# Moving tiles in SBUF: the right heap to 64 modulo 512 bytes, six K and Q buffers to unequal offsets

## The chip, the cores and the metric

One core of a Trainium2 chip runs one program per execution. The metric is the device time in microseconds of that execution, the median over several. TensorE, VectorE, ScalarE and GpSimd each have an instruction queue of their own and meet through semaphores; SyncE issues most DMAs. SBUF has 128 partitions; a tile's address is a byte offset inside each partition, and it is these offsets that the change alters.

## What is computed

One transformer-like block on x of 2048 rows and 448 columns, in float32:

```python
mod = (_silu(c) @ w_mod).reshape(c.shape[0], 6, 1, -1)
sa, ca, ga, sb, cb, gb = (mod[:, 0], mod[:, 1], mod[:, 2], mod[:, 3], mod[:, 4], mod[:, 5])
h = _layernorm(x, axis=-1) * (1 + ca) + sa
x = x + ga * _A_ref(h, A_wqkv, A_wo)
h = _layernorm(x, axis=-1) * (1 + cb) + sb
x = x + gb * _B_ref(h, B_w_in, B_w_sp, B_b_sp, B_w_out)
return x
```

A is attention with 16 heads of 28 columns and a softmax over all 2048 keys. B is a gated MLP: z = gelu(h w_in) is split in two halves of 896 columns, z1 and z2; z2 is normalised over its columns, multiplied along the rows by the 2048x2048 matrix w_sp, shifted by b_sp, multiplied by z1 and projected back to 448 columns by w_out.

## The kernel before

**Matmuls.** TensorE streams a moving operand of up to 512 columns against weights of 128 columns that it has loaded before. Operands are float32r. To keep precision, most are split in a high part and a low remainder, and a product is made of several matmuls: 11 steps for a 448-row contraction (the pairs in STEPS), three for the spatial product and for the output projection. In the attention, K and Q carry both parts on different rows, so that one matmul of 84 or 86 rows does it all.

**Tiles and where they stand.** Pools allocate from the left end of SBUF upward or, with side="right", from the right end downward. heapD (84 KB per partition, L67) is the first and topmost tile on the right. It holds in turn: hT (the first normalised input, transposed) and wqk (weights of the Q and K projection); OT (the attention's output) and wos; w2, most of z2, and uT (the gated result). Below it on the right lie the stage tiles (qf, qh, ql, osb, rb) and, early, wv. On the left lie the constants (ident, ones, spread and small ones), V, the early loads, and for the attention the pool stk with the six buffers kst0 to kst2 and qst0 to qst2 of 8 KB each (L329), then npool and ppool with the probabilities P. After the attention the left holds heapA (w1, later z2), heapB (h2T, later z2), two more heaps, and the tiles of w_sp (wsp_h, wsp_l). Each allocation is rounded up to 32 bytes, so that a tile's address is the sum of the sizes before it.

**Stages, in the order of time.**
1. To about 92 us: modulation, first layer norm, V (v_tiles, L261: weights from hT, moving wv) and the first Q and K projections (qk_unit, L270: weights wqk, moving hT).
2. To 165 us: the remaining 20 units of L270, with one m product (below) put before steps 1, 4, 7 and 10 of each.
3. To 893 us: attention. The loop runs over u = 16 heads x 16 key tiles. For each u it issues four s products (s_mm, L420: weights a 128-key slice of K, moving a 512-query slice of Q), each followed by an m product (m_mm, L389: weights a 128-query slice of Q, moving a 512-key slice of K) for the unit 20 ahead, hence for the next head or the one after. VectorE takes the row maximum of each m result (L394), ScalarE the exponential of each s result into P (L424). After every second u come eight products with V (pv_mm, L435). Head h uses kst and qst number h mod 3. The ring of seven PSUM tiles is shared by s and m. The last 20 u have no m products any more.
4. Normalisation of a head: its output is copied to osb (tag qf, two buffers), the sums are inverted, osb is scaled and scattered to OT by DMAs (n_scatter, L472). The last head goes another way: a matmul with spread as weights spreads its sums (L673), and VectorE inverts and scales (L675, L676).
5. To 938 us: output projection (wo_mm, L600: weights OT, moving wos), second layer norm. To 1012 us: z1 (L712: weights w1 in heapA, moving h2T). To 1083 us: z2 (L774: weights h2T, moving w2 in heapD).
6. To the end: the spatial product in four blocks of 512 columns (mix_part, L820 to L822: weights the 128-column slices of z2, 8 of 16 tiles in heapD, 4 each in heapA and heapB; moving wsp_h, wsp_l, wsp_h), and between its steps the projection of the block before (y_part, L860 to L862: weights uT in heapD, moving wouts).

The order on each engine is written out by hand (the schedule is manual); tiles only wait for the last use of the slot that they take.

Of the kernel before, what the change touches and what calls it, by code (L numbers as in the profile page):

```python
# [8 lines left out]
F32 = mybir.dt.float32  # L9
F32R = mybir.dt.float32r  # L10
# [6 lines left out]
S, D, H, DH, FH = 2048, 448, 16, 28, 896  # L17
# [16 lines left out]
def tile_adaln_mha_gmlp(ctx, tc, x, wqkv, wo, w_in, w_spT, b_sp, w_out, cT, w_mod, out):  # L34
    nc = tc.nc
    ctx.enter_context(tc.manual_schedule())
    pe, dve, act, pool, sp = nc.tensor, nc.vector, nc.scalar, nc.gpsimd, nc.sync

    const = ctx.enter_context(tc.tile_pool(name="const", bufs=1))
    dpool = ctx.enter_context(tc.tile_pool(name="dpool", bufs=1, side="right"))  # L40
# [8 lines left out]
    ident = const.tile([128, 128], F32, name="ident")  # L49
    make_identity(nc, ident)  # L50
    ones = const.tile([128, 128], F32, name="ones")
    dve.memset(ones, 1.0)

    spread = const.tile([128, 128], F32, name="spread")
    dve.tensor_copy(
        spread.rearrange("p (a b) -> p a b", b=32),
        ident.rearrange("p (a b) -> p a b", b=32)[:, :, 28:29].broadcast_to([128, 4, 32]),
    )
    mhalf = const.tile([128, 4], F32, name="mhalf")
    dve.memset(mhalf, -0.5)  # L60
    silu = const.tile([112, 4], F32, name="silu")
# [3 lines left out]
    bcs = {"gb": const.tile([128, D], F32, name="bc_gb")}  # L65

    heapD = dpool.tile([128, 24 * 896], F32R, name="heapD")  # L67

    def hview(heap, off, a, b):
        return heap[:, off : off + a * b].rearrange("p (a b) -> p a b", b=b)  # L70
# [11 lines left out]
    def weight_part(dst, i, raw, hi_eng, lo_eng, zero=True):  # L82

        n = raw.shape[-1]
        h = dst[:, i if i < 3 else 6, :n]
        if hi_eng is act:
            act.activation(h, raw, AF.Copy)
        else:
            hi_eng.tensor_copy(h, raw)
        if i < 3:  # L90
            sub(lo_eng, dst[:, 3 + i, :n], raw, h)
        else:
            sub(lo_eng, dst[0:64, 7, :n], raw[0:64], h[0:64])
            if zero:
                pool.memset(dst[64:128, 7, :n].bitcast(F32), 0.0)
# [6 lines left out]
    def ln_transpose(xns, full_pool, dsts, scol, bcol, engs, los=(pool,) * 4, mid=None, after=None):  # L102

        tps = []
        for c in range(4):
            tp = ring.tile([128, 512], F32, name="tp", tag="s")
            tps.append(tp)
            for t in range(4):
                pe.transpose(tp[:, t * 128 : (t + 1) * 128], xns[t][:, c * 128 : (c + 1) * 128], ident)  # L109
        if mid:  # L110
            mid()
        for c in (0, 2, 1, 3):
            tp = tps[c]
            f = full_pool.tile([128, 512], F32, name="hfull")
            if engs[c] is act:
                act.activation(f, tp, AF.Identity, scale=scol[:, c : c + 1], bias=bcol[:, c : c + 1])
            else:
                engs[c].tensor_scalar(
                    out=f, in0=tp, scalar1=scol[:, c : c + 1], scalar2=bcol[:, c : c + 1], op0=ALU.mult, op1=ALU.add
                )  # L120
            hi = dsts[:, c if c < 3 else 6, :]
            if engs[c] is act:
                act.activation(hi, f, AF.Copy)
            else:
                engs[c].tensor_copy(hi, f)
            if c < 3:
                sub(los[c], dsts[:, 3 + c, :], f, hi)
            else:
                sub(los[c], hi[64:128], f[64:128], hi[64:128])
            if after:  # L130
                after(c)
# [9 lines left out]
    stage = stg.enter_context(tc.tile_pool(name="stage", bufs=2, side="right"))  # L141
# [12 lines left out]
    def load_mod(pair, eng):  # L154
        for k in range(4):
            wms[pair, k] = e1.tile([112, 2, D], F32, name="wm", bufs=4)
            eng.dma_start(wms[pair, k], w_mod[:, pair, k])

    def load_x(g, eng):
        xg = e1.tile([128, 4, D], F32, name="xg")  # L160
        for t0, t1 in ((0, 1), (1, 2), (2, 4)) if g == 0 else ((0, 4),):
            eng.dma_start(xg[:, t0:t1, :], x[g, :, t0:t1])
        for t in range(4):
            xts[4 * g + t] = xg[:, t, :]
# [60 lines left out]
    def ln_stats(g):  # L225
        mv = e1.tile([128, 4, 2], F32, name="mv")
        sts = []
        for t in range(4):
            st = e1.tile([128, 6], F32, name="st", bufs=4)
            dve.bn_stats(out=st, in_=xts[4 * g + t])  # L230
            sts.append(st)
        for t in range(4):
            dve.bn_aggr(out=mv[:, t, :], in_=sts[t])
        rs = e1.tile([128, 4], F32, name="rs")
        rstd_of(mv[:, :, 1], rs, 4)
        mv1[g] = (mv, rs)
# [19 lines left out]
    def v_tiles(*kts):  # L256
        pvs = [ring.tile([128, 512], F32, name="pv", tag="s") for _ in kts]
        for j, (a, b) in enumerate(STEPS):
            for kt, pv in zip(kts, pvs):
                g, t = divmod(kt, 4)  # L260
                pe.matmul(pv[:, :D], hT[g][:, a, t * 128 : (t + 1) * 128], wv[:, b, :], start=j == 0, stop=j == NST - 1)  # L261
        for kt, pv in zip(kts, pvs):
            dve.tensor_copy(V[:, kt, :, 0:DH], pv[:, :D].rearrange("p (h d) -> p h d", d=DH))

    def qk_unit(m, g, mid=None):
        pq = ring.tile([128, 512], F32, name="pq", tag="s")
        for j, (a, b) in enumerate(STEPS):
            if mid and j in mid:
                mid[j]()
            pe.matmul(pq, wqk[:, b, m * 128 : (m + 1) * 128], hT[g][:, a, :], start=j == 0, stop=j == NST - 1)  # L270
        f = stage.tile([128, 512], F32, name="qf")
        act.activation(f, pq, AF.Copy)  # L272
        hi = stage.tile([128, 512], F32R, name="qh")
        act.activation(hi, f, AF.Copy)
        lo = stage2.tile([128, 512], F32R, name="ql")
        sub(pool, lo, f, hi)
        for i, t in enumerate((hi, lo)):
            sp.dma_start(qk_scr[i][m * 128 : (m + 1) * 128, g * 512 : (g + 1) * 512], t.bitcast(F32))
# [42 lines left out]
    for g in range(NG):  # L321
        if g + 2 < NG:
            load_x(g + 2, sp)
        if g in (0, 2):
            load_mod(1 + g // 2, sp)
        if g == 3:
            early.close()
            stk = att.enter_context(tc.tile_pool(name="stk", bufs=1))
            kq = [[stk.tile([128, S], F32R, name=f"{n}st{i}") for n in "kq"] for i in range(3)]  # L329
            kst, qst = [a[0] for a in kq], [a[1] for a in kq]  # L330
            npool = att.enter_context(tc.tile_pool(name="npool", bufs=2))

            def load_head(h, c0=0, c1=S):
                k, q = kst[h % 3], qst[h % 3]
                if h < 2 and c0 == 0:
                    pool.memset(k[64:86, :].bitcast(F32), 1.0)
                for r0, i in ((0, 0), (56, 1), (28, 0)):
                    sp.dma_start(k[r0 : r0 + 28, c0:c1].bitcast(F32), qk_scr[i][D + h * DH : D + (h + 1) * DH, c0:c1])
                for r0, i in ((0, 0), (28, 1), (56, 0)):
                    sp.dma_start(q[r0 : r0 + 28, c0:c1].bitcast(F32), qk_scr[i][h * DH : (h + 1) * DH, c0:c1])  # L340

            load_head(0, 0, 1536)
            for m in (0, 3):
                qk_unit(m, g)
            load_head(0, 1536, S)
        if g == 0:
            v_tiles(0, 1)
            v_tiles(2)
        else:
            v_tiles(4 * g)  # L350
            v_tiles(4 * g + 1)
        if g == 0:
            for i in range(4):
                weight_part(wqk, i, raws.pop(("qk", i)), act, (dve, pool)[i % 2], False)
        if g + 1 < NG:
            ln_transpose(xns, e1, hT[g + 1], cols["ca"], cols["sa"], (act,) * 4)
        if g + 2 < NG:
            ln_stats(g + 2)
            xns = ln_norm(g + 2)
        if g > 0:  # L360
            v_tiles(4 * g + 2)
        else:
            pool.memset(V[:, :, :, DH:32], 1.0)
        v_tiles(4 * g + 3)
        if g == 2:
            mod_bc("ga", accs[1][:, 0, :])
            mod_col(("sb", accs[1][:, 1, :], 0.0))
        if g < 3:
            for m in (0, 3):
                qk_unit(m, g)  # L370
        if g in (1, 2):
            for k in range(4):
                mod_acc(g, k)
# [289 lines left out]

    HELD = 7
    x_load(0)
    for i in range(4):
# [11 lines left out]
    for i in range(2):  # L680
        win_prep(0, i, pool)
    for t in range(1, HELD):
        wo_mm(t, STEPS_MAIN)
    for qb in range(4):
        o_split(3, qb, dve if qb % 2 == 0 else pool)
    for i in range(2, 4):
        win_prep(0, i, pool)
    for t in range(HELD):
        wo_mm(t, STEPS_Z)
# [247 lines left out]
```

## Time and profile before

| | us |
|---|---|
| median of 3 runs | 1469.54 (1468.12 to 1470.2) |
| the profiled execution | 1468.3 |
| its span, first to last instruction | 1466.5 |
| granted TensorE clock | 0.999 of full |
| TensorE busy | 1440.9 |
| VectorE busy | 882.5 |
| ScalarE busy | 733.0 |

How to read what follows. In groups of instructions the number behind the comma is the mean duration of one in ns, behind the bar the idle time before them. Matmuls overlap: the next one starts before the recorded end of the last, so the distance between starts says more than a duration. In the chain in order of time a row is start, length, engine, tile, line and a count. In the view of one line, three numbers with slashes are minimum, median and maximum duration in ns. PEld rows are weight loads; q behind an engine's name means its queue.

### The profile page before, as it was taken

How to read it: one execution, taken by the hardware profiler on the slowest of the kernel's cores; microseconds unless marked ns; L12 is line 12 of the kernel's file. 1: busy time of each engine (PE TensorE's matmuls, PEld its weight loads, DVE VectorE, ACT ScalarE, POOL GpSimd, SP SyncE). 2: the span in 40 equal slices, each digit the busy share in tenths (PEclk: the TensorE clock that was granted, in tenths of full speed). 3: DMA queues.
4: the chain of work that ended last, by engine and by line, in shares of the span. 5: the costliest groups of instructions: out<-in, count | busy, mean ns of one | idle time of the engine just before them, and what ended most of it. 6: DMA issues, size and time to landing. Idle time of an engine off the chain costs nothing.

```text
span 1466.5 us, 19636 instructions
## 1 busy us (share of the span) xinstructions
PE 1440.9 (98%) x7314; PEld 1016.6 (69%) x7314; DVE 882.5 (60%) x1440; ACT 733.0 (50%) x1390; POOL 301.3 (21%) x273
## 2 busy tenths in 40 slices
PE   6999999999999999999999999999999999999999
PEld 5887655555555555555555556888988888888887
DVE  6657888888888888888888823911542411414114
ACT  3523576776776776777677695542432201212111
POOL 5734200000011012001000012511663400302002
PEclk9999999999999999999999999999999999999999
DMA  7563401221022221221112005332003422313223
GB/s 214 149 179 146 137 19 36 52 53 40 17 50 53 54 51 28 52 53 46 34 27 52 15 24 165 139 141 86 15 21 96 127 69 77 101 65 96 81 69 107
DMA packets 56132, 111.24 MB, mean 76 GB/s; under 512 B 11900, under 2 KB 22780, under 8 KB 53516
## 3 DMA queue, kind: packets, MB, share of 16 engines
q1 hardware_dynamic: 55868, 109.76, 25.5%
q8 instruction: 57, 0.93, 0.3%
q14 instruction: 39, 0.32, 0.1%
q10 hardware_dynamic: 168, 0.23, 0.1%
HBM read 75.89 MB, written 29.48 MB: 72 GB/s over the span
## 4 chain that ended last, share of the span: by engine, by line
PE 94%; DVE 2%; DMA 2%; issue 1%; POOL 1%; SPq 0%; ACT 0%; DVEq 0%; POOLq 0%; ACTq 0%
PE st_ps L420 18%; PE mt L389 16%; PE o_ps L435 16%; PE acc L820 7%; PE acc L822 7%; PE acc L821 7%; PE pq L270 5%; PE z_ps L774 5%; PE z_ps L712 5%; PE pv L261 2%; PE y_ps L861 2%; PE y_ps L862 2%; PE y_ps L860 2%; PE tp L109 1%; DMA wm<-in_w_mod_dram 1%
## 5 line engine op out<-in xcount | busy, mean ns | idle before, releaser
L394 DVE TENSOR_REDUCE pm<-mt 128x1 f32<-128x512 f32 x1024 | 632.3, 683 | 121.0 <-PE mt L389 120.6
L424 ACT ACTIVATE P<-st_ps 128x512 f32<-128x512 f32 x1024 | 514.2, 621 | 153.6 <-PE st_ps L420 153.2
L420 PE MATMUL st_ps<-qst,kst 86*128 86x512 f32 x1024 | 410.4, 412 | 0.0
L389 PE MATMUL mt<-kst,qst 84*128 84x512 f32 x1024 | 405.8, 396 | 0.3 <-DVE pm L394 0.3
L420 PEld LDWEIGHTS st_ps<-qst,kst 86*128 86x128 f32 x1024 | 192.9, 189 | 145.1 <-issue 82.1
L435 PE MATMUL o_ps<-P,V 128*32 128x512 f32 x2048 | 247.5, 599 | 0.0
L389 PEld LDWEIGHTS mt<-kst,qst 84*128 84x128 f32 x1024 | 194.9, 190 | 37.2 <-DVE pm L394 0.7
L76 DVE TENSOR_TENSOR wsp_l<-raw_sp,wsp_h 128x512 fp32r<-128x512 f32 x64 | 52.2, 818 | 188.7 <-ACT wsp_h L757 188.7
L757 ACT ACTIVATE wsp_h<-raw_sp 128x512 fp32r<-128x512 f32 x64 | 40.3, 630 | 233.7 <-DMA raw_sp<-in_w_spT_dram 189.7
L435 PEld LDWEIGHTS o_ps<-P,V 128*32 128x32 f32 x2048 | 54.2, 109 | 123.5 <-issue 116.2
L76 POOL TENSOR_TENSOR heapD<-u,heapD 128x512 fp32r<-128x512 f32 x27 | 44.7, 1690 | 258.0 <-ACT heapD L839 172.9
L461 POOL TENSOR_TENSOR osb<-osb,rb 128x512 f32<-128x512 f32 x15 | 19.2, 1279 | 353.2 <-ACT P L424 191.8
L270 PE MATMUL pq<-heapD 128*128 128x512 f32 x308 | 87.4, 402 | 2.9 <-DVE heapD L76 2.9
L820 PE MATMUL acc<-wsp_h,heapD 128*128 128x512 f32 x224 | 89.1, 398 | 0.7 <-DVE u L837 0.7
L822 PE MATMUL acc<-wsp_h,heapD 128*128 128x512 f32 x224 | 88.6, 396 | 0.0
L821 PE MATMUL acc<-wsp_l,heapD 128*128 128x512 f32 x224 | 88.2, 394 | 0.0
L270 PEld LDWEIGHTS pq<-heapD 128*128 128x128 f32 x308 | 59.2, 193 | 17.1 <-DVE heapD L76 3.4
L76 POOL TENSOR_TENSOR nl<-nf,nh 16x128 fp32r<-16x128 f32 x16 | 7.2, 450 | 281.2 <-issue 149.1
L865 DVE TENSOR_TENSOR x2t<-x2t,y_ps 128x448 f32<-128x448 f32 x12 | 7.5, 621 | 75.9 <-PE y_ps L862 75.9
L272 ACT ACTIVATE qf<-pq 128x512 f32<-128x512 f32 x28 | 16.7, 597 | 66.9 <-PE pq L270 66.9
L820 PEld LDWEIGHTS acc<-wsp_h,heapD 128*128 128x128 f32 x224 | 42.1, 188 | 10.9 <-DVE u L837 1.8
L822 PEld LDWEIGHTS acc<-wsp_h,heapD 128*128 128x128 f32 x224 | 42.1, 188 | 10.4
(150 smaller groups left out, 1686.0 us busy)
## 6 DMA issues: line engine op xcount, KB each, us to landing
raw_sp<-in_w_spT_dram SPq DMA_DIRECT2D x64, 256.0 KB
kst<-qk_scr SPq DMA_DIRECT2D x45, 224.0 KB
qst<-qk_scr SPq DMA_DIRECT2D x45, 224.0 KB
qk_scr<-qh SPq DMA_DIRECT2D x28, 256.0 KB
qk_scr<-ql SPq DMA_DIRECT2D x28, 256.0 KB
z_scr<-z1t SPq DMA_DIRECT2D x28, 256.0 KB
z<-z_scr SPq DMA_DIRECT2D x28, 256.0 KB
wm<-in_w_mod_dram SPq DMA_DIRECT2D x12, 392.0 KB
```

The lines of the kernel that those rows point to most:

```text
L76: eng.tensor_tensor(out=dst, in0=a, in1=hi.bitcast(F32), op=ALU.subtract)
L270: pe.matmul(pq, wqk[:, b, m * 128 : (m + 1) * 128], hT[g][:, a, :], start=j == 0, stop=j == NST - 1)
L389: pe.matmul(mt, qst[h % 3][0:84, t * 128 : (t + 1) * 128], kst[h % 3][0:84, kb * 512 : (kb + 1) * 512], start=True, stop=True)
L394: dve.tensor_reduce(out=pms[h][:, t, kb : kb + 1], in_=mt, axis=AX.X, op=ALU.max)
L420: pe.matmul(st, kst[h % 3][0:86, kt * 128 : (kt + 1) * 128], qst[h % 3][0:86, qb * 512 : (qb + 1) * 512], start=True, stop=True)
L424: act.activation(p, st, AF.Exp, scale=SCALE)
L435: pe.matmul(otile[h][32 * qb : 32 * qb + 32, :], V[:, kt, h, :], ptiles.pop((u, qb)), start=kt == 0, stop=kt == NT - 1)
L712: pe.matmul(ps_t, w1[:, b, f * 128 : (f + 1) * 128], h2T[g][:, a, :], start=j == 0, stop=j == NST - 1)
L774: pe.matmul(ps_t[:, :D], h2T[g][:, a, tt * 128 : (tt + 1) * 128], w2[:, b, hf * D : (hf + 1) * D], start=j == 0, stop=j == NST - 1)
L820: pe.matmul(acc[f], z2[st][:, 0, fs], hi, start=st == 0, stop=False)
L821: pe.matmul(acc[f], z2[st][:, 0, fs], lo, start=False, stop=False)
L822: pe.matmul(acc[f], z2[st][:, 1, fs], hi, start=False, stop=st == NT - 1)
```

## The change

spread is no longer a constant but takes a qf slot of the stage pool, and the copy that fills it stands just before the last part of the attention's tail. A tile of 416 bytes that nothing uses is put behind heapD, which lowers heapD and all that stands below it on the right by as much. The six K and Q buffers come in another order, with unused tiles of 256, 64, 32 and 32 bytes between them. No instruction but the copy is moved; sizes and values stay the same.

```diff
@@ -50,12 +50,6 @@
-    spread = const.tile([128, 128], F32, name="spread")
-    dve.tensor_copy(
-        spread.rearrange("p (a b) -> p a b", b=32),
-        ident.rearrange("p (a b) -> p a b", b=32)[:, :, 28:29].broadcast_to([128, 4, 32]),
-    )
@@ -65,6 +59,7 @@
     heapD = dpool.tile([128, 24 * 896], F32R, name="heapD")
+    dpool.tile([128, 104], F32, name="padD")
@@ -326,8 +321,12 @@
             stk = att.enter_context(tc.tile_pool(name="stk", bufs=1))
-            kq = [[stk.tile([128, S], F32R, name=f"{n}st{i}") for n in "kq"] for i in range(3)]
-            kst, qst = [a[0] for a in kq], [a[1] for a in kq]
+            kq = {}
+            for i, (nm, pad) in enumerate((("k0", 64), ("q0", 0), ("q2", 16), ("k2", 0), ("q1", 8), ("k1", 8))):
+                if pad:
+                    stk.tile([128, pad], F32, name=f"pad{i}")
+                kq[nm] = stk.tile([128, S], F32R, name=f"{nm[0]}st{nm[1]}")
+            kst, qst = ([kq[f"{n}{i}"] for i in range(3)] for n in "kq")
             npool = att.enter_context(tc.tile_pool(name="npool", bufs=2))
@@ -663,6 +662,12 @@
+    spread = stage.tile([128, 512], F32, name="spread", tag="qf")[:, 0:128]
+    dve.tensor_copy(
+        spread.rearrange("p (a b) -> p a b", b=32),
+        ident.rearrange("p (a b) -> p a b", b=32)[:, :, 28:29].broadcast_to([128, 4, 32]),
+    )
     HELD = 7
```

## The prediction

> **What bounds the kernel now.** I read the page first, for which engine ends the time.
>
> ```profile
> span 1466.5 us, 19636 instructions
> ...
> PE 1440.9 (98%) x7314; PEld 1016.6 (69%) x7314; DVE 882.5 (60%) x1440; ACT 733.0 (50%) x1390; POOL 301.3 (21%) x273
> ...
> PEclk9999999999999999999999999999999999999999
> ...
> PE 94%; DVE 2%; DMA 2%; issue 1%; POOL 1%; SPq 0%; ACT 0%; DVEq 0%; POOLq 0%; ACTq 0%
> ```
>
> TensorE is on the chain that ended last for 94% of the span, at the full granted clock. The change adds and removes no matmul. So the question is whether one matmul follows the last any sooner when its operands stand at other addresses. That needs the distance from one start to the next, which the chain in order of time gives. First z1 and z2:
>
> ```profile
> 957.63 54.90 PE z_ps L712 x242
> 1012.53 70.43 PE z_ps L774 x352
> ```
>
> 54.90/242 = 0.2269 us for 512 columns, 70.43/352 = 0.2001 us for 448. Nothing in this trace holds a steadier or lower pace, so I call these the floors. Now the spatial product of the gMLP, three matmuls (L820 to L822) per 128x512 tile; the rows are each third matmul, the first two and the last of a stretch with weights from heapD, then the ends of one with weights from heapB:
>
> ```profile
> 1082.95 0.24 PE acc L820
> 1083.65 0.24 PE acc L820
> ...
> 1121.45 0.24 PE acc L820
> ```
>
> ```profile
> 1440.21 0.23 PE acc L820
> ...
> 1444.97 0.23 PE acc L820
> ```
>
> Over heapD it is 38.50/55 = 0.700 us for three, over heapB 4.76/7 = 0.680 us. Same instructions, same moving tiles, same engines around them: only the place of the weights differs. A third of 0.020 us is 6.7 ns per matmul. I call that one slip.
>
> Where do the operands stand? Adding up tile sizes in the order of allocation (each rounded up to 32 bytes): heapA, heapB, the later heaps, wsp_h and wsp_l are at 64 modulo 512 bytes; heapD at 480 (the change's words give 64 after, and padD is 104 x 4 = 416 bytes lower); all six K and Q buffers at 320, which is 64 modulo 256. Every slice taken as weights begins a multiple of 512 bytes on, so it keeps its buffer's offset. 480 is not a multiple of 64; 64 and 320 are.
>
> **The change: heapD.** Recorded ends lie about 0.16 us beyond the next start (390 ns recorded against a step of 227), so differences of recorded durations are differences of pace. Groups by line and shape, mean ns behind the comma:
>
> ```profile
> L820 PE MATMUL acc<-wsp_h,heapD 128*128 128x512 f32 x224 | 89.1, 398 | 0.7 <-DVE u L837 0.7
> L822 PE MATMUL acc<-wsp_h,heapD 128*128 128x512 f32 x224 | 88.6, 396 | 0.0
> L821 PE MATMUL acc<-wsp_l,heapD 128*128 128x512 f32 x224 | 88.2, 394 | 0.0
> L820 PE MATMUL acc<-wsp_h,heapA 128*128 128x512 f32 x112 | 43.7, 390 | 0.0
> L861 PE MATMUL y_ps<-heap,heapD 128*128 128x448 f32 x112 | 41.2, 368 | 0.0
> L774 PE MATMUL z_ps<-heapD,heapB 128*128 128x448 f32 x176 | 35.4, 363 | 0.0
> ```
>
> Lines as minimum/median/maximum ns, L270 before and after line 389 joins it, L389 in the second stretch:
>
> ```profile
> L600 PE MATMUL wo_ps<-heapD x176: 358/368/767, 893.1 to 938.5; 128*128 128x448 f32 x176
> L261 PE MATMUL pv<-wv,heapD x176: 358/367/474, 23.0 to 92.4; 128*128 128x448 f32 x176
> L270 PE MATMUL pq<-heapD x44: 387/389/504, 73.5 to 83.4; 128*128 128x512 f32 x44
> L270 PE MATMUL pq<-heapD x219: 387/395/744, 94.0 to 164.6; 128*128 128x512 f32 x110
> L389 PE MATMUL mt<-kst,qst x80: 393/401/497, 94.6 to 164.8; 84*128 84x512 f32 x80
> ```
>
> Moving data from heapD costs nothing (L774 runs at its floor of 363 with w2 there); weights from heapD do. After the change they stand where heapA's stand:
>
> - acc: (8 + 6 + 4) ns x 224 = 4.0 us; I take 3.9 for the 390 that is sometimes 391.
> - y: three lines at about 5 ns x 112 each = 1.6 us.
> - wo: 5 ns x 176 = 0.9, of which some 65 run before 908 us beside the wait for the last head's normalisation and are worth nothing: 0.6.
> - pv: 4 ns x 176 = 0.7, less the first ones that wait for loads: 0.6.
> - Q/K projection with m products between: 6 ns x 220 = 1.3, and m there 401 against 396 later, 5 ns x 80 = 0.4: 1.7.
>
> Sum **8.4 us**, nearly all on TensorE's own chain. One row speaks against it: L270 in 73.5 to 83.4 us takes weights at 480 with a median of 389, the floor. There weights and moving operand share the offset; in acc they don't (64 against 480). So an odd weight address by itself is not enough, and the y, wo and pv terms, whose offset differences do not change into acc's new one, could come to nothing (5.6 us left). If it were the differences of 0 and 256 that cost in wo, z2 would get these and lose 5 ns x 352 = 1.8 us (3.8 left). I keep 8.4, because the rows with weights at 64 (acc over heapA and heapB, z1, z2) never show a slip.
>
> **The change: K and Q.** From the sizes the buffers go to 64 (k0, q0), 128 (q2, k2), 160 (q1) and 192 (k1) modulo 256. The s product of a head streams its Q while the m product's weights, Q of the next head or the one after, are loaded; m streams a later K while K of the head is loaded. All these pairs have equal offsets now and unequal ones afterwards.
>
> ```profile
> L389 PE MATMUL mt<-kst,qst x1024: 389/396/497, 94.6 to 850.4; 84*128 84x512 f32 x171
> L420 PE MATMUL st_ps<-qst,kst x880: 392/396/506, 199.9 to 839.5; 86*128 86x512 f32 x176
> L420 PEld LDWEIGHTS st_ps<-qst,kst x880: 185/190/195, 200.1 to 839.8; 86*128 86x128 f32 x176
> L420 PE MATMUL st_ps<-qst,kst x55: 388/393/502, 861.7 to 887.0; 86*128 86x512 f32 x55
> L420 PEld LDWEIGHTS st_ps<-qst,kst x53: 186/188/190, 861.9 to 886.7; 86*128 86x128 f32 x53
> ```
>
> ```profile
> 336.82 0.40 PE L389 MATMUL mt<-kst,qst 84*128 84x512 f32 x1
> ...
> 340.09 0.39 PE L389 MATMUL mt<-kst,qst 84*128 84x512 f32 x1
> ```
>
> The last fence is one train of s and m: 14 steps in 3.27 us, 0.2336 each, again one slip over 0.2269. Nothing in the trace shows K and Q at unequal offsets, so I bound it. Best: every slip goes, 6 to 6.7 ns x some 1,900 (without those that open a train) = 12 us gained. Worst: a second slip each, 2,048 x 6.7 = 13.7 us lost; the pair "m, then projection" at unequal offsets has 401, nearly two slips. Between: where s runs alone (861.7 us on) the offsets are just as equal, yet it runs at 393 and its weight loads at 188 instead of 190. So about half the excess needs no change of offset to vanish, and offsets can be blamed for the other half, 6 us. Weights from q1, at 160, would again stand off a multiple of 64; they feed a third of the m products, a sixth of all. 5/6 of 6 is **5 us**, which I take: near the middle of ends far apart.
>
> ```profile
> L394 DVE TENSOR_REDUCE pm<-mt 128x1 f32<-128x512 f32 x1024 | 632.3, 683 | 121.0 <-PE mt L389 120.6
> L424 ACT ACTIVATE P<-st_ps 128x512 f32<-128x512 f32 x1024 | 514.2, 621 | 153.6 <-PE st_ps L420 153.2
> ```
>
> Both consumers sit idle waiting for these products, 121 and 154 us in total, so neither becomes late by a gain of 5 to 12 us. P moves by 128 bytes; V's weight slices stand 128 bytes apart by head, so P meets the same set of differences as before: nothing.
>
> **The change: spread.** It leaves VectorE's start and comes back before the last head's sums.
>
> ```profile
> L55 DVE COPY spread<-ident x1: 573/573/573, 1.3 to 1.3; 128x128 f32<-128x128 f32 x1
> 872.65 6.41 SPq L472 DMA_DIRECT2D heapD<-osb  x8
> 894.81 0.40 PEld L673 LDWEIGHTS sums<-osb,spread 128*128 128x128 f32 x2
> 896.12 3.36 DVE L675 RECIPROCAL rb<-sums 128x512 f32<-128x512 f32 x1 [31.28 <-PE sums L673]
> ```
>
> At the start VectorE then waits for ScalarE's first result anyway: nothing. At the end the copy adds a wait: its slot was osb of head 14, free when the eight scatters issued from 872.65 to 879.06 have landed. Only the reciprocal is queued behind it on VectorE, idle for 31.28 us and waiting for sums at 895. The 0.57 us has some 14 us of cover: nothing. Without that cover it would be 0.6 us straight on the way to the last scatter.
>
> **Sum.** 8.4 + 5 = 13.4 us. The profiled execution took 1468.3 us (1.8 around its span): 1454.9. The median of the runs is 1.2 above it: **1456 us**.
>
> **The rivals.**
> - K and Q lose every slip, as acc over heapA shows for products with company: 1469.5 - 8.4 - 12 = 1449. For it: z2 runs at its floor with unequal offsets. Against it: s alone at 393.
> - K and Q gain nothing, with q1's weights paying up to 5 ns x 320 = 1.6: 1461 to 1463. For it: z1 and acc over heapA have equal offsets and no slip, so equality isn't the fault; rows of 84 and 86 in turn could be.
> - Slower: unequal offsets cost K and Q a second slip, as in "m, then projection" (401): 1469.5 - 8.4 + 13.7 = 1475. It decides from 8.4/2,048 = 4.1 ns per product.
> - The change does not do what it says: the slip comes from something else that goes with heapD, and the time stays at 1469.5. For it only the floor of L270 at 480.
>
> The Trainium skill, SBUF — State Buffer, Who interferes with whom, says that PE never waits on anyone and names only the port pair of VectorE and GpSimd as contended. By that rule the sum is nothing and this last rival holds. The trace disagrees as far as 0.700 against 0.680 goes.
>
> **How the numbers follow.** Forecast (K and Q gain 2 to 9; 1451 to 1460) 0.36; every slip gone 0.22; K and Q unmoved 0.27; second slip 0.09; no effect 0.06. The range takes the first three, out to 1447 and 1465, which leaves 0.15 or a little more outside. A measurement tells some 0.2% (2.9 us) from no change. Faster: the first three, 0.85; same: no effect and a hair of the others, 0.07; slower: 0.08.
>
> **What would show it.** L820 to L822 over heapD at 390 and 0.68 us for three; y at 363; wo, pv near 363; L270 beside L389 near 390; z2 still 363. If y and wo keep 368 while acc falls, the difference of offsets counts, not the weights' own. L389 and L420 at about 393 for the forecast, 390 for the first rival, 396 for the second, 402 for the slower one. L389 with weights from q1 slower than from q0 and q2 would confirm the multiple of 64. I am wrong altogether if L820 over heapD stays at 398.

## The result and the profile after

| | before | after |
|---|---|---|
| median of 20 runs each, same chip, us | 1469.01 (1467.33 to 1471.68) | 1466.32 (1464.62 to 1469.84) |
| ratio after / before | | 0.9984 [0.9977, 0.9991] |
| the profiled execution, us | 1468.3 | 1466.46 |

Faster, by 2.7 us and not by 13: the direction was right, and the time lies 1.3 us above the range. From here on lines are those of the kernel after: pv L256, pq L265, m L388, s L419, wo L599, z1 L717, z2 L779, acc L825 to L827, y L865 to L867.

The page of after: TensorE still ends the time, at the full granted clock.

```profile
span 1464.7 us, 19637 instructions
...
PE 1436.5 (98%) x7314; PEld 1015.3 (69%) x7314; DVE 884.6 (60%) x1440; ACT 733.1 (50%) x1390; POOL 302.0 (21%) x273
...
PEclk9999999999999999999999999999999999999999
...
PE 92%; DVE 2%; POOL 2%; DMA 2%; issue 1%; ACT 0%; SPq 0%; ACTq 0%; DVEq 0%; POOLq 0%
```

The chain in order of time (start, length, line, count):

```profile
960.23 54.87 PE z_ps L717 x242
1015.10 71.34 PE z_ps L779 x352
1086.43 0.23 PE acc L825
1087.13 0.23 PE acc L825
...
1123.85 0.23 PE acc L825
```

The spatial product over heapD now does its three in (1123.85 - 1086.43)/55 = 0.680 us instead of 0.700. z1 is as it was. But z2, which stood at its floor, takes 71.34 us for the same 352 products instead of 70.43.

Groups by line and shape (mean ns behind the comma), then single lines (minimum/median/maximum ns; L265 and L388 are the stretch from 96 to 167 us, L419 the one with m between and then alone):

```profile
L825 PE MATMUL acc<-wsp_h,heapD 128*128 128x512 f32 x224 | 87.6, 391 | 0.6 <-DVE u L842 0.6
L827 PE MATMUL acc<-wsp_h,heapD 128*128 128x512 f32 x224 | 87.3, 390 | 0.0
L826 PE MATMUL acc<-wsp_l,heapD 128*128 128x512 f32 x224 | 87.2, 389 | 0.0
L865 PE MATMUL y_ps<-heap,heapD 128*128 128x448 f32 x112 | 40.8, 365 | 0.0
```

```profile
L779 PE MATMUL z_ps<-heapD,heapB x176: 362/365/369, 1014.9 to 1050.4; 128*128 128x448 f32 x176
L599 PE MATMUL wo_ps<-heapD x176: 362/366/765, 895.8 to 941.1; 128*128 128x448 f32 x176
L256 PE MATMUL pv<-wv,heapD x176: 358/367/575, 21.8 to 94.6; 128*128 128x448 f32 x176
L265 PE MATMUL pq<-heapD x219: 388/395/742, 96.1 to 166.4; 128*128 128x512 f32 x110
L388 PE MATMUL mt<-kst,qst x80: 392/395/499, 96.7 to 166.7; 84*128 84x512 f32 x80
L419 PE MATMUL st_ps<-qst,kst x881: 389/397/502, 200.8 to 841.8; 86*128 86x512 f32 x177
L419 PE MATMUL st_ps<-qst,kst x53: 387/393/504, 864.0 to 889.0; 86*128 86x512 f32 x53
```

acc over heapD reached 390 as forecast. y came down half the way (368 to 365), z2 rose from 363 to 365, pv stayed at 367, and s, with its 396 before and 397 now, gained nothing. A train of s and m reads like this in the timeline of after (14 steps from the first row to the last):

```profile
338.94 0.39 PE L388 MATMUL mt<-kst,qst 84*128 84x512 f32 x1
...
342.20 0.40 PE L388 MATMUL mt<-kst,qst 84*128 84x512 f32 x1
```

3.26/14 = 0.2329 us a step, against 0.2336 before: the slip is still there.

Where the time went, by starts of the lines named (us). "Early" ends where the third group of Q/K projections begins; "attention" is first s to last s. Runs named here are told below.

| run | early | Q/K and m | attention | z2 | first acc to end | span |
|---|---|---|---|---|---|---|
| before | 94.0 | 71.3 | 724.6 | 70.43 | 383.7 | 1466.5 |
| after | 96.1 | 71.0 | 725.5 | 71.34 | 378.4 | 1464.7 |
| spread alone | 94.0 | 71.3 | 724.6 | 70.43 | 384.1 | 1466.6 |
| heap alone | 95.4 | 71.0 | 724.5 | 71.34 | 379.3 | 1463.5 |
| K and Q alone | 95.2 | 71.2 | 725.3 | 70.43 | 383.2 | 1467.5 |
| 84 rows | 95.6 | 71.3 | 723.1 | 70.43 | 384.2 | 1467.7 |
| 86 rows | 97.7 | 73.5 | 720.4 | 70.43 | 384.5 | 1468.7 |
| 86 rows, K and Q | 94.4 | 73.3 | 721.9 | 70.43 | 384.7 | 1467.8 |
| wsp at 480 | 95.8 | 71.3 | 724.8 | 70.43 | 384.4 | 1469.5 |
| shifted heap | 97.1 | 71.0 | 724.6 | 70.43 | 378.3 | 1463.9 |
| last version | 94.1 | 71.0 | 719.9 | 70.43 | 379.9 | 1457.9 |

Between before and after: early +2.1, Q/K -0.3, attention +0.9, z2 +0.9, acc and y -5.3. The early stage varies from 93.5 to 97.7 us between profiles, also where nothing in it was changed (84 rows), so its 2.1 are mostly scatter of one execution. The other columns repeat within some 0.3 us in runs with the same offsets and rows and the same slots of PSUM (0.6 at most, 720.4 and 721.0 in the attention of *86 rows* and *both*); the last one within 1.5 us, once 2.6 (378.3 here and 380.9 in the run *both*, in the same layout).

**A finer measure.** In what follows "excess" is the step from one matmul's start to the next one's, less a floor taken as 226.7 ns for 512 columns and 200.0 for 448 (the prediction's floors, 0.2269 and 0.2001 us, are means over whole stages). It is a mean over all steps with no pause (a step of more than about 30 ns over the floor counts as one), sorted by the buffer being streamed and the weights being loaded beside it (those of the next matmul). D is the streamed operand's offset less that of the weights, modulo 256.

| products | excess before, at D | excess after, at D |
|---|---|---|
| acc over heapD (512 columns) | 6.7 ns, 96 | 0.7, 0 |
| acc over heapA and heapB | 0.7, 0 | 0.6, 0 |
| y (448 columns) | 5.3, 96 | 2.5, 0 |
| z2 | 0.1, 160 | 2.7, 0 |
| wo | 4.3, 0 | 4.1, 0 |
| pv | 3.9, 128 | 3.8, 128 |
| s and m together | 7.5, 0 | 7.6, mixed |

pv and wo have the same difference before and after, since operand and weights moved together, and the same excess, though the weights went from 480 to 64. (wo's mean scatters from profile to profile, 2.5 to 4.3 ns wherever D is 0; pv's lies between 3.7 and 3.9.) z2's weights stand at 64 in both. So the theory after the result is **difference**: the pace hangs on how the streamed operand and the weights loaded beside it stand to each other. Its rival is the prediction's reading, **the weights' own place** (a multiple of 64 is safe). For s and m, where offsets gained nothing, the theory is **rows in turn**: matmuls of 84 and of 86 rows follow each other, and that makes the slip.

### The profile page after: what moved, and what is told of

Its sections match the earlier page's. It is cut to its first block, busy times and chain, and to the rows that moved or that the text cites. A ratio compares the mean times of both kernels' runs of the same rounds, so it can differ in the third digit from the quotient of the medians.

```text
span 1464.7 us, 19637 instructions
## 1 busy us (share of the span) xinstructions
PE 1436.5 (98%) x7314; PEld 1015.3 (69%) x7314; DVE 884.6 (60%) x1440; ACT 733.1 (50%) x1390; POOL 302.0 (21%) x273
## 4 chain that ended last, share of the span: by engine, by line
PE 92%; DVE 2%; POOL 2%; DMA 2%; issue 1%; ACT 0%; SPq 0%; ACTq 0%; DVEq 0%; POOLq 0%
PE st_ps L419 18%; PE mt L388 16%; PE o_ps L434 16%; PE acc L825 7%; PE acc L827 7%; PE acc L826 7%; PE z_ps L779 5%; PE z_ps L717 5%; PE pq L265 4%; PE y_ps L866 2%; PE y_ps L865 2%; PE y_ps L867 2%; PE pv L256 1%; PE tp L104 1%; POOL heapD L71 1%
## 5 line engine op out<-in xcount | busy, mean ns | idle before, releaser
L419 PE MATMUL st_ps<-qst,kst 86*128 86x512 f32 x1024 | 409.8, 411 | 0.0
L388 PE MATMUL mt<-kst,qst 84*128 84x512 f32 x1024 | 406.6, 397 | 0.3 <-DVE pm L393 0.3
L419 PEld LDWEIGHTS st_ps<-qst,kst 86*128 86x128 f32 x1024 | 193.1, 189 | 144.8 <-issue 82.2
L388 PEld LDWEIGHTS mt<-kst,qst 84*128 84x128 f32 x1024 | 194.8, 190 | 38.3 <-DVE pm L393 0.7
L265 PE MATMUL pq<-heapD 128*128 128x512 f32 x308 | 85.8, 396 | 2.9 <-DVE heapD L71 2.9
L825 PE MATMUL acc<-wsp_h,heapD 128*128 128x512 f32 x224 | 87.6, 391 | 0.6 <-DVE u L842 0.6
L827 PE MATMUL acc<-wsp_h,heapD 128*128 128x512 f32 x224 | 87.3, 390 | 0.0
L265 PEld LDWEIGHTS pq<-heapD 128*128 128x128 f32 x308 | 58.0, 189 | 16.4 <-DVE heapD L71 3.4
L825 PEld LDWEIGHTS acc<-wsp_h,heapD 128*128 128x128 f32 x224 | 42.1, 188 | 9.7 <-DVE u L842 1.4
L71 POOL TENSOR_TENSOR ql<-qf,qh 128x512 fp32r<-128x512 f32 x28 | 36.4, 1304 | 59.7 <-ACT qh L269 47.2
```

The source lines that it names most:

```text
L71: eng.tensor_tensor(out=dst, in0=a, in1=hi.bitcast(F32), op=ALU.subtract)
L388: pe.matmul(mt, qst[h % 3][0:84, t * 128 : (t + 1) * 128], kst[h % 3][0:84, kb * 512 : (kb + 1) * 512], start=True, stop=True)
L419: pe.matmul(st, kst[h % 3][0:86, kt * 128 : (kt + 1) * 128], qst[h % 3][0:86, qb * 512 : (qb + 1) * 512], start=True, stop=True)
L825: pe.matmul(acc[f], z2[st][:, 0, fs], hi, start=st == 0, stop=False)
L827: pe.matmul(acc[f], z2[st][:, 1, fs], hi, start=False, stop=st == NT - 1)
```

## The experiments

All are against the kernel before, timed beside them on the same chip.

### The parts one at a time

*spread alone*: the constant becomes a slot of the stage pool; no pads.

> The spread copy moved, no pad anywhere: every offset modulo 512 is as before. Theory A (the time is set by the offsets and nothing else): 1469 us, acc over heapD 398 ns, the same V copies and PE gaps before 95 us as in before. Theory B (the first 95 us got longer in the changed kernel because the copy left VectorE's start and later work then falls together differently): some 2 to 4 us slower than before, with PE waiting for a V copy near 70 us as in the changed kernel.

1469.52 us against 1468.51, ratio 1.0007 [0.9998, 1.0017]; no stage moved. The forecast of nothing holds.

*Heap alone*: spread and the 416 bytes behind heapD.

```diff
     heapD = dpool.tile([128, 24 * 896], F32R, name="heapD")
+    dpool.tile([128, 104], F32, name="padD")
```

> heapD at 64, K and Q all at 320 as before. Theory A (what counts is the difference, modulo 256, between the moving operand and the weights loaded beside it): acc over heapD 390, y 365 to 366, z2 365 to 366 (up from 363), wo and pv unchanged at 367 to 368, the K and Q products at 396: 4 to 5 us gained from 893 us on, total 1465 to 1467. Theory B (weights at an odd multiple of 32 are slow, as the prediction had it): wo, pv and y at 363, z2 stays 363, total near 1461. If the K and Q offsets were harmful in the changed kernel, this one is faster than it by that much.

1465.1 against 1468.51, ratio 0.9974 [0.9965, 0.9984]: as much as the whole change or more. All of the gain lies here.

*K and Q alone*: spread and the new order with pads of the six buffers.

> Only the K and Q buffers at unequal offsets, heapD at 480. Theory A (the slip in the attention does not hang on these offsets): the stretch from 200 to 840 us as long as before within 1 us, the single pairs of buffers faster or slower by up to 3 ns, total 1469 within 1.5. Theory B (unequal offsets help, half of the slips go): 5 us gained, total 1464.

1469.18 against 1468.51, ratio 1.0005 [0.9996, 1.0013]. The attention is 0.7 us longer. By pair the excess in the changed kernel ranges from 5.5 ns (k1 streamed, k0 loaded) to 10.3 (q0 and q1), and here much the same; before, these pairs all had 6.9 to 8.1. What some pairs won, others lost.

The mean hides what made the attention longer, since it leaves out the slowest steps. In after, 40 steps with k2 streamed and k1 loaded stand 33 ns over the floor, and 39 in this run; in before, none of that pair does. One of them in the timeline of after:

```profile
218.52 0.43 PE L388 MATMUL mt<-kst,qst 84*128 84x512 f32 x1
218.78 0.40 PE L419 MATMUL st_ps<-qst,kst 86*128 86x512 f32 x1
```

At 33 ns instead of some 6, 40 such steps cost 1.1 us, about what the attention lost. Why this pair, and why these steps of it, stays open.

*84 rows*: s leaves out the two rows that subtract the row maximum, so that s and m both have 84 rows; the exponential's argument is scaled down for it. The maximum's subtraction is left out.

```diff
-        pe.matmul(st, kst[h % 3][0:86, ...], qst[h % 3][0:86, ...], start=True, stop=True)
+        pe.matmul(st, kst[h % 3][0:84, ...], qst[h % 3][0:84, ...], start=True, stop=True)
```

> The kernel before with the s product on 84 rows instead of 86, as the m product has; this leaves out the subtraction of the row maximum, and the exponential's scale is a thousandth so that it stays finite. Theory A (the slip of s and m comes from 84 and 86 rows taking turns): both fall from 396 to 390, 11 to 13 us gained. Theory B (it does not): 396 and 1469 as before.

1466.22 against 1468.51, ratio 0.9986 [0.9975, 0.9998], with offsets equal as before. The excess of s and m fell from 7.5 to 4.2 ns. The time gained 2.3 us and not the 11 to 13 expected: not every slip goes, and this profile loses some 3.4 us to a dip of the clock inside the attention (last section), so the table shows less than the other runs without the slip. Five of this kernel's ten executions have a mean granted clock of 0.993 to 0.996; the other five, at 0.999, took 1463.8 to 1465.4, with a median of 1464.3, 4.2 us under before.

### Is it the rows?

*86 rows*: m takes the 86 rows as well, with rows 84 and 85 of Q set to zero first, so that nothing is left out.

```diff
+                if c0 == 0:
+                    sp.dma_start(q[84:86, :]..., z2r...broadcast_to([2, S // 64, 64]))
...
-            mt, qst[h % 3][0:84, ...], kst[h % 3][0:84, ...], start=True, stop=True
+            mt, qst[h % 3][0:86, ...], kst[h % 3][0:86, ...], start=True, stop=True
```

> The kernel before, but the m product takes 86 rows as the s product does; rows 84 and 85 of each Q buffer are set to zero by one small DMA per head, so the values stay the same. All offsets as before. Theory 'rows in turn' (the slip of s and m comes from 84 and 86 rows taking turns, not from offsets): the steps of a train fall from 0.2333 to 0.2267 us as with 84 rows, mean excess over the floor from about 7.6 to 4 ns, the attention 5 us shorter, 1464 us. Theory 'the scaled exponential' (what the run with 84 rows gained came from leaving out the maximum or from its other data): steps stay at 0.2333 and the time at 1469; 16 more DMAs could cost a few tenths.

The slip is gone from the steady part of a train. Timeline of this run, eight products of 86 rows on end:

```profile
337.71 0.39 PE L426 MATMUL st_ps<-qst,kst 86*128 86x512 f32 x1
...
339.30 0.39 PE L395 MATMUL mt<-kst,qst 86*128 86x512 f32 x1
```

1.59/7 = 0.2271 us a step. Over the attention the steps in the middle of a train (the fifth to the tenth) take 228.9 ns on average, in before 234.0. The mean excess of s and m is 4.1 ns (most of what is left sits in the first and the last steps of a train, at 232 to 233 ns), the attention 4.2 us shorter. Yet the time is 1468.72 against 1469.57, ratio 0.9996 [0.9985, 1.0008]: 2.2 us were given back in the Q/K stage; the 2 us that this leaves lie at the edge of the interval. Where they went, the run *both* (shifted heap, below, with the 86 rows; 73.2 us in that stage) shows in its timeline:

```profile
122.71 0.40 PE L391 MATMUL mt<-kst,qst 86*128 86x512 f32 x1
122.94 0.63 PE L266 MATMUL pq<-heapD 128*128 128x512 f32 x2
123.89 0.50 PE L391 MATMUL mt<-kst,qst 86*128 86x512 f32 x1 [0.32 <-DVE pm L396]
```

```profile
123.14 0.69 DVE L396 TENSOR_REDUCE pm<-mt 128x1 f32<-128x512 f32 x1 [0.24 <-PE mt L391]
```

The m product at 123.89 waits for the maximum of the m product just before it, which ends at 123.83. It has got the very PSUM slot that this one had. In the compiled program that happens to one m product of this stage in before, and to five of six in a row here: with the added DMA the slots are given out in another order. In this stage m waited for that maximum 1.1 us in before (two waits) and 3.1 us here (six), which is 2.0 of the 2.2 us.

*86 rows, K and Q*: the same with the change's K and Q offsets.

> The K and Q offsets of the change, without its heap part, with the m product on 86 rows, so that the slip of taking turns is gone and only the offsets are left to act. Reference is the run with 86 rows and equal offsets: attention 720.4 us, 3.2 to 4.8 ns over the floor by pair. Theory 'equal offsets are best for 512 columns' (acc: 0 to 1 at a difference of 0, 5 to 7.5 at 96 and 160): now unequal offsets show in full, 2 to 3 ns more in the mean of 2,048 products, the attention 4 to 6 us longer than with 86 rows and equal offsets, 1471 or so in all. Theory 'K and Q do not mind offsets': 720 again, 1469.

1469.35 against 1470.37, ratio 0.9994 [0.9984, 1.0004]. The attention is 1.6 us longer than with 86 rows at equal offsets, the excess of s and m 5.5 ns instead of 4.1. Both theories missed the size, but the sign is that of "equal is best": once the slip is gone, moving K and Q apart costs. It does not cost by D alone: pairs at 64 have 3.5 to 3.8 ns, where equal offsets have 3.2 to 5.0, and pairs at 128 have 4.9 in one case and 7.0 in the other, against 4.8 and 4.1.

### Is it the difference, or the weights' own place?

*wsp at 480*: only the streamed operand of acc is moved, from 64 to 480 modulo 512; all weights stay.

```diff
+    wpad = ctx.enter_context(tc.tile_pool(name="wpad", bufs=1))
+    wpad.tile([128, 104], F32, name="padW")
     wp = ctx.enter_context(tc.tile_pool(name="wp", bufs=2))
```

> The kernel before with wsp_h and wsp_l moved by 416 bytes to 480 modulo 512; heapD stays at 480, heapA and heapB at 64. Theory 'difference': acc over heapD (now difference 0) falls to 390 and 0.680 us for three, though its weights still stand at 480; acc over heapA and heapB (now 160) shows what 160 does to 512 columns, 390 if it is harmless there too. With it harmless 4 us gained, 1465. Theory 'the weights' own offset': acc over heapD stays at 394 to 398, acc over heapA and heapB at 390, 1469.

Groups of this run by line and shape:

```profile
L822 PE MATMUL acc<-wsp_h,heapD 128*128 128x512 f32 x224 | 87.7, 392 | 0.7 <-DVE u L839 0.7
L823 PE MATMUL acc<-wsp_l,heapD 128*128 128x512 f32 x224 | 87.3, 390 | 0.0
L824 PE MATMUL acc<-wsp_h,heapD 128*128 128x512 f32 x224 | 87.2, 389 | 0.0
...
L822 PE MATMUL acc<-wsp_h,heapA 128*128 128x512 f32 x112 | 44.4, 396 | 0.0
L822 PE MATMUL acc<-wsp_h,heapB 128*128 128x512 f32 x112 | 44.4, 396 | 0.0
```

The picture is turned round: over heapD, whose weights still stand at 480, the products are at 390 (excess 0.8 ns), and over heapA and heapB, whose weights stand at the multiple of 64 where they always stood, at 396 (7.5). The rival falls, for 512 columns: weights at 480 and at 64 were each streamed against from 64 and from 480, and both times the equal pair is the fast one. Since heapA and heapB lost what heapD gained, the time is 1470.01 against 1469.57, ratio 0.9998 [0.9987, 1.0009]; that 160 would be harmless for 512 columns was wrong.

*Shifted heap*: heap alone, with wos and w2 160 bytes on, uT 96, and wv at 224, so that all 448-column products have D = 160 as z2 had.

```diff
-    w2 = hview(heapD, 14336, 8, 896)
+    w2 = hview(heapD, 14336 + 40, 8, 896)
```

> The heap part alone (as in the run without the K and Q pads), and wos and w2 160 bytes further on, uT 96 bytes, wv to 224 modulo 512: every 448-column product then has a difference of 160 modulo 256 between the moving operand and the weights loaded beside it, the one of z2 before. Theory 'difference': z2 back from 71.3 to 70.4 us, y, wo and pv at a mean of 363 instead of 366 to 368, acc over heapD stays at 390: 0.9 + 0.8 + 0.7 + 0.6, so 2.5 to 3 us under the heap part alone, 1462. Theory 'the weights' own offset' (a multiple of 64 is safe, anything else slips): uT now stands 32 off a multiple of 64, so y gets slower, and nothing else moves: no gain over the heap part alone, 1465 or more.

Lines of this run, and its chain:

```profile
L596 PE MATMUL wo_ps<-heapD x176: 360/363/768, 895.8 to 941.3; 128*128 128x448 f32 x176
L257 PE MATMUL pv<-wv,heapD x176: 360/363/575, 22.8 to 95.5; 128*128 128x448 f32 x176
```

```profile
1015.36 70.43 PE z_ps L776 x352
```

z2 has its 70.43 back, wo falls to an excess of 0.2 ns and pv to 0.9: with only their weights gone to 64 and D unchanged, wo had stayed within its scatter and pv at 3.8. y, with its weights at 160, stays at 4.1. The time is 1464.69 against 1469.57, ratio 0.9967 [0.9956, 0.9979], by the ratios 1 us under the heap alone, with overlapping intervals, and not 3: z2 gives 0.9 us, pv some 0.5, while wo's 0.7 does not show (from the first wo product to z1 it is 45.7 us, before 45.6), and the profile's early stage was a long one.

*y the other way* (shifted heap, but uT at 64 and wouts 160 bytes on):

> The shifted heap again, but the difference of 160 in y is made the other way: uT back at 64 modulo 512 and the moving wouts 160 bytes further on (224 and 480 modulo 512), as the operands of z2, wo and pv stand. In the run before this one wo and pv went to their floor, y at (moving 64/320, weights 160) did not (4.6 ns over). Theory 'difference and place' (a difference of 160 helps 448 columns only with the weights at a multiple of 64): y falls to its floor, 336 x 4.6 ns = 1.5 us under the shifted heap, 1463. Theory 'y is special' (its three products in turn with acc cost it something whatever the offsets): y stays 4 to 5 ns over, 1464.7.

1465.46 against 1470.37, ratio 0.9969 [0.9956, 0.9981]; excess of y 3.0 and 4.0 for its two kinds of offset. Neither expectation quite: y gets to its floor in no layout tried, and its best is D = 0 with 2.5. What else it wants stays open.

### The parts put together

*Both* (shifted heap and 86 rows):

> The shifted heap and the m product on 86 rows together. If both theories (difference of offsets for the 448-column products and acc, rows in turn for s and m) hold and their gains add: 7 us for the heap and 4 to 5 for the rows, 1457 to 1459. If the rows' gain was not real: 1462. If neither: 1465.

1464.0 against 1469.57, ratio 0.9957 [0.9943, 0.997]; 2.2 us short for the slots told above and 2.6 us for a longer last stage (380.9 against 378.3 in the same layout).

*The same with zeros from memory clears* (for the first three heads) and y as in *y the other way*:

```diff
                     pool.memset(k[64:86, :].bitcast(F32), 1.0)
+                    pool.memset(q[64:86, :].bitcast(F32), 0.0)
+                if h > 2:
+                    sp.dma_start(q[84:86, :]..., z2r...broadcast_to([2, S // 64, 64]))
```

> The same with the m product on 86 rows; the rows of zeros for the first three heads now come from memory clears on GpSimd instead of a DMA, which leaves the order in which PSUM slots are taken near that of before (each m waits for the maximum of two m products back at the least; with the DMA it was the one just before). Theory 'rows in turn': the attention is 4 us shorter as in both runs with 86 rows, and the 2.2 us that these lost between the first s and the Q/K projection do not come back: 1459. Theory 'the 2.2 us belong to the 86 rows': 1461 with y at its floor.

1462.24 against 1470.37, ratio 0.995 [0.9935, 0.9964]. The Q/K stage is back at 71.0 us and the attention at 719.9, and m's waits are 1.1 us in two again, so the 2.2 us were the slots and not the rows. The last stage, at 382.0, took the rest.

*Last version*: wouts back, so that y and acc have D = 0.

> Each part as it measured best: heap, w2, wos, wv and 86 rows as in the run before this one, but wouts back at 64 and 320 modulo 512, with uT at 64 (the difference of the changed kernel, 0 modulo 256). Neither way of giving y a difference of 160 had brought it to its floor: 4.6 ns over with (moving 64/320, weights 160), 3 to 4 with (224/480, 64), against 2.2 to 2.8 at 0. Theory 'y and acc are best at 0': y back at 2.2 to 2.8, acc at 0.5 to 1, from the first acc to the end 378.4 to 379.3 us as in the two runs that have that layout, against 382.0: 3 us gained, 1459.5. Theory 'that stage scatters from one program to the next': 380 to 382 as before, 1462.

```profile
span 1457.9 us, 19664 instructions
...
L423 PE MATMUL st_ps<-qst,kst 86*128 86x512 f32 x1024 | 407.5, 409 | 0.0
L392 PE MATMUL mt<-kst,qst 86*128 86x512 f32 x1024 | 403.3, 394 | 0.3 <-DVE pm L397 0.3
```

1459.56 against 1469.83, ratio 0.993 [0.9915, 0.9945]: 10 us under the kernel before, and some 7 to 8 under the change, by medians and by ratios of different sessions. Of the median, what was expected came. The last stage, at 379.9 us, lies between the two expectations; 2.0 us under the run before it is no more than that stage scatters (*y the other way*, with the layout of the run before it, has 380.2), so what y's layout gave is not shown by the time.

## Why the prediction was wrong

By its own steps:

- **acc, 3.9 us**: the size was right: 6.0 ns x 672 = 4.0, and shown in the chain. The reason given, the weights' own place, was not: the run with wsp at 480 has the same 390 ns with these weights still at 480. The size came out because the change also brought D from 96 to 0.
- **y, 1.6**: 0.9 came ((5.3 - 2.5) x 336), with D gone from 96 to 0.
- **wo and pv, 0.6 each**: nothing came. The weights moved to 64, the difference stayed.
- **z2, nothing**: 0.9 lost. The text had this case (differences of 0 and 256 cost in wo, so z2 would get them) and priced it at 1.8, but did not take it.
- **Q/K projection with m, 1.7**: 0.3. Only the step from m to the projection got faster (10.0 to 6.3 ns, D from 96 to 0). The step back, from the projection to m, went from a D of 160 to 0 in most cases and became slower, 3.5 to 4.5 ns, and so it is in every profile with heapD at 64. The projection's own steps stayed at 5 to 6 ns though their D is 0 in both; matmuls of 84 and 128 rows follow each other there, but no run tested that.
- **K and Q, 5**: 0.9 lost. The sign named for the multiple of 64, m with weights from q1 slower, did not come: 395 ns against 397 with q0 and 399 with q2. The steps beside which q1 is loaded were slower (9.5 against 7.3 ns), but not with rows alike (5.2 against 5.0 and 5.7).
- **spread, nothing**: right.

Two steps failed. The first is "offsets can be blamed for the other half, 6 us". The row it was drawn from, s alone at 393 with offsets just as equal, said something else: alone, s is followed by s, of 86 rows each. The rival "rows of 84 and 86 in turn could be" was the right one for K and Q, at 1461 to 1463, and had 0.27. The runs with 84 and 86 rows bear it out: 3.4 ns of the 7.5 go with the rows, and with rows alike unequal offsets only cost (5.5 against 4.1 ns).

The second is the reason for keeping 8.4: "the rows with weights at 64 (acc over heapA and heapB, z1, z2) never show a slip". All of these rows also had a difference of 0 with 512 columns, or 160 with 448 (z2). The row against it, L270 at the floor with weights at 480 and an equal offset, was quoted and then outvoted. Taken as the rule, with a cost at 0 and 256 for 448 columns, it would have left 3.8 us by the prediction's own prices, near the 4.3 that the heap's terms came to (4.0 + 0.9 + 0.3 - 0.9). With nothing from K and Q, 1469.5 - 3.8 = 1465.7 is already over the upper end of the range, 1465; the 0.9 that K and Q lost takes it to 1466.6, and 1466.3 was measured.

The range was too narrow because the two doubts were priced apart and never together.

The Trainium skill, SBUF — State Buffer, Who interferes with whom, calls TensorE's two SBUF reads, moving operand and weight load, independent, and says that PE never waits on anyone. The run with wsp at 480 disagrees: 390 against 396 ns in one and the same stage, turned round by moving the streamed operand alone.

What is shown is the dependence on the difference and on the rows. What it is in the memory or in TensorE that makes it so was not measured. Nor is D alone the whole law. For 448 columns 160 is the floor for z2 and wo and near it for pv, whose weights stand at 64, and not for y. For 512 columns 0 is best for acc, but the steps from the projection to m and the single pairs of K and Q do not follow D.

## What to carry to other kernels

Where TensorE is the bound, subtract the best step in the trace from every other step and sort by the pair of streamed operand and next weights; a few ns times thousands of products is the gain at hand, and the pair, not one address, is what to lay out (here a difference of 0 for acc, 160 modulo 256 for z2, wo and pv). It paid here to give matmuls that take turns the same number of rows, even though two of them are zeros. After any edit, look whether the order in which PSUM slots are given out has changed: here that took back half of a real gain.

## What the runs showed of the hardware that was not expected

**The cost of taking turns.** 84 rows after 86 and back cost about 5 ns a matmul in the middle of a train (234.0 ns a step in before; 229.0 with all on 84, 228.9 with all on 86), and in the two trains shown 6.5 (0.2336 against 0.2271 us).

**A clock dip with TensorE at work.** Windows of 8 us in the run with 84 rows, then in before (TensorE busy and count first, granted clock in the third column from the end):

```profile
172.00:180.00 8.00, 8.00 (x29) 3.47 (x28) 3.68 (x7) 3.03 (x6) 0.00 (x0) 0.57 0.75 156
```

```profile
172.00:180.00 8.00, 8.00 (x51) 4.09 (x51) 6.13 (x11) 4.75 (x10) 0.00 (x0) 1.00 0.55 118
```

For some 8 us the clock stood at 0.57, with 29 matmuls where before has 51; 8 x 0.43 = 3.4 us are lost. TensorE had been busy for 7.79 of the 8 us before, so no long pause stands ahead of the dip; what started it stays open. The page's row of 40 slices showed nothing of it.

**VectorE and GpSimd in each other's way.** In after, early on (DVE, then POOL, then TensorE waiting for the copy behind them):

```profile
63.29 6.24 DVE L201 SCALAR_TENSOR_TENSOR acc<-wm,silu,acc 112x896 f32<-112x896 f32 x3
```

```profile
65.19 6.85 POOL L71 TENSOR_TENSOR heapD<-hfull,heapD 128x512 fp32r<-128x512 f32 x4 [0.79 <-ACT heapD L118]
```

```profile
70.12 3.46 PE L256 MATMUL pv<-wv,heapD 128*128 128x448 f32 x11 [3.00 <-DVE V L258]
```

In before the same three VectorE instructions took 4.44 us, where GpSimd's subtractions began only at 67.89, towards their end:

```profile
64.32 4.44 DVE L206 SCALAR_TENSOR_TENSOR acc<-wm,silu,acc 112x896 f32<-112x896 f32 x3
```

The Trainium skill, SBUF — State Buffer, Who interferes with whom, has a rule for it: a VectorE instruction with two inputs in SBUF contends with a GpSimd instruction that reads SBUF. The 6.24 against 4.44 us agree. It goes with the scatter of the early stage: in the seven profiles with 4.43 to 4.44 us for these three instructions that stage took 93.5 to 95.8 us, in the three with 6.21 to 6.24 us 96.1 to 97.7. Why they meet in one execution and not in another was not followed up.
